# A planned attention-and-MLP kernel: engine time and result time held apart in the planner, a price for a change of matmul kind, and refitted constants

## The chip, the cores and the metric

The kernel runs on one core of one Trainium2 chip. The metric is the device time of one execution in microseconds; lower is better. An execution is one program; nothing is computed on the host but changes of layout.

## The reference

Four sequences of 448 tokens go through attention with 12 heads of 64, whose scores are mixed across heads before the softmax and again behind it, and then through two gated MLPs.

```python
scores = scale * q @ k.T                                   # (4, 12, 448, 448)
scores = einsum('bhij,hg->bgij', scores, w_pre)
attn = softmax(scores, -1)
attn = einsum('bhij,hg->bgij', attn, w_post)
x = (attn @ v), heads side by side                         # (1792, 768)
h = x @ w_in; x = (h * clip(h + 3, 0, 6) / 6) @ w_out      # d_ff 2048
x = (((x @ w1) * (x @ w2)) @ w3) @ w_out2                  # d_ff 1024
```

## The kernel before, in words

**Attention.** Query rows are cut into 16 chunks (four per sequence). For each chunk, six PE operations `scores` (two heads each) write products of q and k into PSUM; ACT or DVE copies them out into a tile `s`. For sequences 1 to 3, q and k are first split into a high and a low part by POOL (`halve`), and a scores operation is six matmuls; for sequence 0 it is two pairs. The mixes across heads work on groups of ten query rows; two groups make a slot, and there are 23 slots per sequence, 92 in all. In each slot `mix` (L460 on) does this: POOL zeroes four rows of a gather tile `g` (L472); SP issues two gathers from `s` (L481); PE multiplies by the first mixing matrix, `premix`, eight matmuls of 448 columns on 64x64 pieces of the array; DVE takes the row maximum (L495); ACT takes two exponentials with their sums (L501); POOL or DVE adds a small number to the sum, DVE takes the reciprocal and weighs the second mixing matrix with it (L517); PE does `postmix`, 64 matmuls of 60 columns; ACT and DVE copy the result into `pth` or `ptl` (L343, L345). At the end of each of eight units, `values` multiplies by v in three groups of two PE operations, 16 matmuls each. All these products take their place in four PSUM tiles (`pp`), and there are four gather tiles and four tiles `e` for the exponentials.

**The MLPs.** Here PE runs full 128x128 matmuls of 448 columns, three for each product of fp32 values split into high and low parts (`act`, `block`, `wide`, `wo`, `wb` and so on). Where two sequences are taken together, `seven` forms a 2x2 block product from seven products, with sums on DVE (`plus`, L833). The third and the fourth weight of the second MLP are multiplied with each other first (`product34`). Intermediate results go to HBM and back.

**The planner.** Nothing in this order is written out by hand. `Plan.add` collects operations with an engine (or a choice of two), a duration in ns, a priority (smaller is more urgent), what they depend on and what buffers they need. `Plan.run` then plays them through as events: whenever an engine is free, it takes the ready operation with the best priority whose buffers have room, and the kernel issues the instructions on each engine in that order. So durations, delays between engines (`HOP`, `DMA_START`, `DMA_END`, `FREED`) and the priorities' constants (`URGE`) decide the order of every queue, SP's with the DMAs among them. The chip then runs each queue in order, with its real times. The thresholds `p...` in `URGE` say how long the first engine of a choice must still be busy before the second takes the operation. `apart` keeps post-mixes from starting closer than a given time.

In the kernel before, an operation holds its engine until its result is there (`free[e] = end = now + ...`), all PE operations are alike, and PE takes the best ready one.

Of the kernel before, what the change touches and what calls it, by code (L numbers as in the profile page):

```python
# [62 lines left out]
URGE = dict(pPool=13.287, pACT=19737.186, pDVE=67509.792, pOut=3.743, pGuard=376.043, pCopy=12.835, pRest=101.643, pEvac=52.694, load0=33.466, load=-4.77, gather=-168.494, pre=-140.104, max=-8.516, exp=27.495, norm=15.87, post=2.04, evac=43.38, values=32.185, step=8.267, vload=-54.801, vload0=-30.207, lead=-15.369, begin=-9.6, consts=-75.04, moe=104.397, rows=-53.563, win=-87.391, wout=-22.784, w34=71.001, w2=99.201, unit0=3.845, unit1=6.717, down1=95.531, unit2=13.151, down2=98.964, wo=-75.16, wd=-84.964, narrow=-61.372, sums=107.353, w34us=69.981, pHalf=621.884, halve=10.141, gsum=3.533, joined=24.31, pairs=-7.78, lag=-72.907, mix=92.823, wo1=32.07)  # L63
# [26 lines left out]
class Plan:  # L90


    HOP = dict(Host=0, PE=200, ACT=150, DVE=130, Pool=130, SP=0)
    DMA_START, DMA_END, FREED = 1100, 910, 180
# [4 lines left out]
    def add(self, eng, ns, prio, emit, use=(), new=(), part=(), after=(), hold=(), read=(), chain=None, gives=None, wait=None, issue=580, port=False, apart=0):  # L99

        choice = eng if isinstance(eng, dict) else {eng: ns}
        op = dict(choice=choice, eng=None, prio=round(prio, 6), emit=emit, new=list(new), id=len(self.ops), gives=gives or {}, chain=chain, issue=issue, apart=apart, port=("Pool", "DVE") if port else ("Pool",))
# [12 lines left out]
        return op  # L118
# [12 lines left out]
    def run(self):  # L131
# [14 lines left out]
        wire = port = burst = 0.0  # L146
        freed = deque()
        events = [(0.0, -1)]
        order = []
        while events:  # L150
            now, done = heapq.heappop(events)
            if done >= 0:
                op = self.ops[done]
                for tag, n in op["gives"].items():
                    self.room[tag] += n
                for x in op["holds"]:
                    x.held -= 1
                    if not x.held:
                        freed.append((now + self.FREED, x.tag))
# [17 lines left out]
            for e, heap in waiting.items():  # L177
                if free[e] > now:
                    continue
                skipped = []  # L180
                while heap:
                    prio, i = heapq.heappop(heap)
                    op = self.ops[i]
                    if op["eng"]:
                        continue
                    first = next(iter(op["choice"]))
                    homes = None
                    if op["ready"] <= now and (e == first or free[first] > now + URGE["p" + op["wait"]]) and (port <= now or e not in op["port"]) and (not op["apart"] or burst <= now):
# [28 lines left out]
                    break  # L217
# [12 lines left out]
def attention_moe(ctx: ExitStack, tc, qd, kd, vd, consts, w_in, w_out, w1, w2, w3t, w4, out):  # L230
# [197 lines left out]
    def scores(prio, ci, hp):  # L428
# [20 lines left out]
        if b:  # L449
            op = plan.add("PE", 660, prio, emit, new=(p, *dest), hold=(st, qh, ql, kh, kl), after=(*ks[hp % 2 * 2:][:2], qs[hp * len(qs) // 6], *after))  # L450
        else:
            op = plan.add("PE", 950, prio, emit, read=(q, k), new=(p, *dest), hold=(st,), after=after)
# [9 lines left out]
    def mix(s):  # L462
# [10 lines left out]
        blanked = plan.add("Pool", 900, at + URGE["gather"] - 1, blank, new=(g,))  # L473
# [17 lines left out]
        plan.add("PE", 900, at + URGE["pre"], premix, use=(g,), new=(pre, e))  # L491
# [10 lines left out]
        for a_ in range(2):  # L502
            plan.add("ACT", 850, at + URGE["exp"], lambda a_=a_: softexp(a_), use=(pre, m, e, *((z,) if a_ else ())), new=() if a_ else (z,))
# [33 lines left out]
        op = plan.add("PE", 1020, at + URGE["post"], postmix, apart=2400, use=(e, w), new=(post, *dest), hold=(pt,), after=() if first else (pt.first,))  # L537
# [12 lines left out]
        for a_ in range(2):  # L550
            op = plan.add({"ACT": 575, "DVE": 645}, 0, at + URGE["evac"], lambda eng, a_=a_: evac(eng, a_), read=(post,), after=pt.writers[-1:] if a_ else (), hold=(pt,), wait="Evac")
            pt.writers.append(op)

    def values(prio, u, hq):
# [4 lines left out]
        for pr in range(2):  # L559
# [6 lines left out]
            plan.add("PE", 1600, prio, emit, read=(pt, v), new=() if pr else (p,), use=(p,) if pr else ())  # L566
# [116 lines left out]
    class Line:  # L683


        def weight(self, prio, src, dst=None, begun=(), raws="raw", ws="w", keep=False):
# [57 lines left out]
            plan.add({"ACT": 150 + n * 5 // 6, "DVE": 150 + n * 52 // 100}, 0, prio, high, read=(m,), new=(h, l), chain=ws if ws in ("wo", "wd") else "w", wait="Copy", port=True)  # L744
# [5 lines left out]
        def mixed(self, prio, got):  # L750
# [16 lines left out]
            for o in "cdba":  # L767
# [5 lines left out]
                a = plan.add({"ACT": 150 + n * 5 // 6, "DVE": 158 + n * 52 // 100}, 0, prio, high, after=(split[o],), new=(q,), hold=(names[o][0],), chain="w", wait="Copy", port=True)  # L773
# [96 lines left out]
    def pair_rows(prio):  # L870

        made = [(Buf("bh"), Buf("bh")) for i in range(7)]
        for c in range(KC // 2):
# [14 lines left out]
            def divide(i, n, where=where, wrote=wrote, part=part, c=c):  # L888
# [6 lines left out]
                one = plan.add({"ACT": 150 + S * 5 // 6, "DVE": 158 + S * 52 // 100}, 0, prio + c, high, after=(*wrote[n], *h.writers[:1]), new=() if c else (h, l), hold=(where[n][0], h, l), chain=None if c else "x", wait="Copy", port=True)  # L895
# [142 lines left out]
    def down(prio, dur, b, ws, graw, loaded, finish, begin, early):  # L1038
# [5 lines left out]
        for n, (k, m) in enumerate(seq):  # L1044
# [28 lines left out]
            ops.append(plan.add("PE", 607 * 4, at, emit, read=(*ws[2 * k], *ws[2 * k + 1], gh, gl), new=() if k else (p,), use=(p,) if k else (), after=() if k else (begin,)))  # L1073
# [21 lines left out]
    def combine(where, wrote, kind, n, when):  # L1095
# [7 lines left out]
        def split(o):  # L1103
# [5 lines left out]
            one = plan.add({"ACT": 150 + n * 5 // 6, "DVE": 150 + n * 52 // 100}, 0, at, high, after=wrote[o], new=(h, l), hold=(where[o][0],), chain="x", wait="Copy", port=True)  # L1109
# [92 lines left out]
    def split(prio, n, x, part, bufs, fh, fl):  # L1202
# [4 lines left out]
        one = plan.add({"ACT": 150 + n * 5 // 6, "DVE": 158 + n * 52 // 100}, 0, prio, high, after=x.writers[:1], new=bufs, hold=(x,), chain="w", wait="Copy", port=True)  # L1207
# [152 lines left out]
```

## Time and profile before

| | us |
|---|---|
| runs shown (3) | 1206.04, 1210.46, 1213.14 |
| median | 1210.46 |
| span of the profiled execution, first to last instruction | 1205.8 |
| PE busy in that span | 1175.1 (97%) |
| DVE / ACT / POOL busy | 826.0 / 625.6 / 198.0 |

The time of the profiled execution as a whole isn't given apart from its span; the span lies 0.2 us under the fastest and 4.7 us under the median run. Engines: PE is the matmul engine (TensorE), PEld its weight loads, DVE is VectorE, ACT ScalarE, POOL GpSimd, SP SyncE, which issues the DMAs. All matmuls are issued by one helper (L238), so they are told apart by the tiles they write and read: `sc` are scores, `pre` and `post` the two mixes, `val` values, `up`, `dn` and `w` the MLPs.

### The profile page before, as it was taken

The page shows a single profiled execution, that of the slowest core. Times are in us where ns is not written, and L with a number is a line of the kernel's source. Part 1 is how long each engine was busy: PE and PEld are TensorE (multiplying, and loading weights), DVE is VectorE, ACT ScalarE, POOL GpSimd, SP SyncE. Part 2 cuts the span into 40 slices and gives each one's busy share as a digit, 9 for nine tenths or more (in the row PEclk, how much of TensorE's full clock was granted, in tenths as well). Part 3 has the DMA queues.
Part 4 walks back from the last instruction along what each step waited for, and adds up shares of the span by engine and source line. Part 5 has one row for each costly group of instructions (what it writes and reads, how often), then busy time and mean ns, then how long its engine had stood idle before and what let it go on. Part 6 is the DMA issues. An engine that isn't in the chain of part 4 may idle for free.

```text
span 1205.8 us, 29514 instructions
## 1 busy us (share of the span) xinstructions
PE 1175.1 (97%) x11904; PEld 975.3 (81%) x11904; DVE 826.0 (68%) x1372; ACT 625.6 (52%) x1196; POOL 198.0 (16%) x411
## 2 busy tenths in 40 slices
PE   8999999999989999999999999999999999998998
PEld 3656665666658899999999999998899998997987
DVE  3877677776688888747855456676864578578592
ACT  7767566566666566535545443432443343334452
POOL 2575564753231000000000000000000000000000
PEclk9999999999999999999999999999999999999999
DMA  6654754745845565846989787998875438396641
GB/s 221 203 175 165 231 183 137 239 144 175 253 148 170 172 217 197 268 145 199 342 287 307 254 284 273 353 313 297 289 232 155 131 124 297 115 286 234 194 149 62
DMA packets 132945, 259.87 MB, mean 216 GB/s; under 512 B 11880, under 2 KB 75208, under 8 KB 132808
## 3 DMA queue, kind: packets, MB, share of 16 engines
q1 hardware_dynamic: 132808, 257.98, 64.7%
q8 instruction: 94, 1.54, 0.6%
q14 instruction: 43, 0.35, 0.1%
HBM read 151.97 MB, written 67.26 MB: 182 GB/s over the span
## 4 chain that ended last, share of the span: by engine, by line
PE 82%; DMA 7%; DVE 3%; ACT 3%; issue 2%; POOL 2%; SPq 2%; POOLq 0%; ACTq 0%; DVEq 0%
PE up L238 40%; PE dn L238 20%; PE w L238 6%; PE post L238 5%; PE sc L238 4%; PE val L238 4%; PE pre L238 4%; DMA g<-s 2%; DMA first<-w_in 1%; SPq L481 1%; DMA xdram<-x 1%; ACT e L501 1%; DMA qraw<-qd 1%; ACT ptl L343 1%; DMA kraw<-kd 1%
## 5 line engine op out<-in xcount | busy, mean ns | idle before, releaser
L238 PE MATMUL up<-act,block 128*128 128x448 f32 x1008 | 206.0, 366 | 5.1 <-DVE v L833 5.1
L238 PEld LDWEIGHTS up<-act,block 128*128 128x128 f32 x1008 | 190.0, 189 | 20.6 <-DVE v L833 5.8
L238 PE MATMUL dn<-gs,act 128*128 128x448 f32 x720 | 147.9, 367 | 0.0
L238 PEld LDWEIGHTS dn<-gs,act 128*128 128x128 f32 x720 | 135.2, 188 | 12.1
L238 PE MATMUL up<-act,wide 128*128 128x448 f32 x630 | 142.8, 368 | 2.0 <-POOL act L241 1.6
L238 PEld LDWEIGHTS post<-wt,e 60*64 60x64 f32 x5760 | 100.9, 135 | 50.3 <-issue 23.0
L501 ACT ACTIVATE e<-pre,m 128x448 f32<-128x448 f32 (+1 forms) x184 | 116.5, 636 | 36.5 <-DVE m L495 20.2
L495 DVE TENSOR_REDUCE m<-pre 128x2 f32<-128x896 f32 (+1 forms) x92 | 99.9, 1086 | 45.4 <-PE pre L238 45.2
L238 PEld LDWEIGHTS up<-act,wide 128*128 128x128 f32 x630 | 117.9, 188 | 13.7 <-POOL act L241 2.1
L709 ACT ACTIVATE raw<-raw 128x384 f32<-128x384 f32 (+1 forms) x140 | 72.5, 524 | 87.4 <-DMA raw<-w 37.8
L238 PE MATMUL post<-wt,e 60*64 60x60 f32 x5760 | 107.5, 220 | 6.4 <-ACT pth L343 1.6
L343 ACT CAST block<-raw 128x384 fp32r<-128x384 f32 x103 | 52.8, 514 | 110.0 <-PE up L238 72.7
L238 PE MATMUL pre<-g,wih 64*64 64x448 f32 x720 | 93.2, 562 | 4.5 <-issue 2.6
L472 POOL MEMSET g<- 4x896 f32 x92 | 76.6, 835 | 110.5 <-PE pre L238 85.4
L238 PE MATMUL up<-act,wb 128*128 128x448 f32 x432 | 89.5, 366 | 0.6 <-DVE v L833 0.5
L238 PEld LDWEIGHTS up<-act,wb 128*128 128x128 f32 x432 | 80.9, 188 | 8.4 <-DVE v L833 0.9
L241 DVE TENSOR_TENSOR block<-raw,block 128x384 fp32r<-128x384 f32 x112 | 60.5, 553 | 30.2 <-ACT block L343 30.1
L833 DVE TENSOR_TENSOR t<-up,t 128x448 f32<-128x448 f32 x60 | 37.2, 621 | 60.3 <-PE up L238 59.4
L238 PE MATMUL dn<-gs,wo 128*128 128x448 f32 x336 | 74.2, 367 | 0.0
L717 ACT ACTIVATE raw<-raw 128x768 f32<-128x768 f32 (+1 forms) x70 | 55.6, 795 | 32.0 <-DVE raw L715 31.9
L721 DVE SCALAR_TENSOR_TENSOR raw<-raw 128x384 int32<-128x384 int32 (+1 forms) x140 | 68.3, 525 | 1.2
L238 PEld LDWEIGHTS dn<-gs,wo 128*128 128x128 f32 x336 | 63.1, 188 | 5.9
(136 smaller groups left out, 1811.6 us busy)
## 6 DMA issues: line engine op xcount, KB each, us to landing
g<-s SPq DMA_DIRECT2D x180, 210.0 KB
raw<-w SPq DMA_DIRECT2D x48, 384.0 KB
graw<-g1dram SPq DMA_DIRECT2D x32, 448.0 KB
raw<-w_out SPq DMA_DIRECT2D x32, 384.0 KB
raw<-w_in SPq DMA_DIRECT2D x28, 384.0 KB
g1dram<-t SPq DMA_DIRECT2D x24, 448.0 KB
raw<-w3t SPq DMA_DIRECT2D x32, 256.0 KB
wraw<-w34dram SPq DMA_DIRECT2D x30, 256.0 KB
```

What stands on the lines that cost most here:

```text
L238: nc.tensor.matmul(o, lhsT=lt, rhs=rh, start=start, stop=stop, **kw)
L241: eng.tensor_tensor(out=o, in0=a, in1=b, op=ALU.subtract)
L343: nc.scalar.copy(o, i)
L472: nc.gpsimd.memset(g.t[:BEFORE], 0.0)
L481: nc.sync.dma_start(out=g.t[BEFORE:BEFORE + 2 * ROWS, y], in_=st.t[p0:p0 + 9 * d + 1:d])
L495: nc.vector.tensor_reduce(out=m.t[used], in_=pre.t[used, :, :S], axis=AX.X, op=ALU.max, negate=True)
L501: nc.scalar.activation(out=e.t[used, a_], in_=pre.t[used, a_, :S], func=ACTF.Exp, bias=m.t[used, a_:a_ + 1], accum_out=z.t[used, a_:a_ + 1])
L709: nc.scalar.mul(value()[:, halves[i]], f(bits(i))[:, :, 1], 2.0 ** -112)
L717: nc.scalar.activation(out=f(y), in_=f(y), func=ACTF.Prelu, alpha=-2.0 ** 32)
L721: two(out=m.t[:, halves[i]], in0=bits(i)[:, :, 0], scalar=29, in1=m.t[:, halves[i]], op0=ALU.logical_shift_right, op1=ALU.bitwise_or)
L833: return plan.add("DVE", 620, prio(at), lambda: nc.vector.tensor_tensor(out=x.t[:, k], in0=o(), in1=x.t[:, k], op=ALU.add), after=after, h ...
```

## The change

Planner: each engine has now a `LAG`, the part of a duration by which the engine is free before the result counts as there; the hops are shorter accordingly. Each PE operation has a kind (`mode`): 1 for scores, 2 for both mixes, 3 for values, 0 for the rest. An operation of another kind than the one before takes 105 ns more (`SWITCH`). When PE is free, the planner takes the best ready operation; if it is of another kind, it looks on for a ready one of the same kind with a priority at most `stay` worse, and takes that. The distance of post-mixes, 2400 ns before, is now the constant `apart`. Durations of single operations are changed, and all constants of `URGE` have new values. No operation is added or removed, and no instruction's operands are changed.

```diff
-URGE = dict(pPool=13.287, pACT=19737.186, pDVE=67509.792, pOut=3.743, pGuard=376.043, pCopy=12.835, pRest=101.643, pEvac=52.694, load0=33.466, load=-4.77, gather=-168.494, pre=-140.104, max=-8.516, exp=27.495, norm=15.87, post=2.04, evac=43.38, values=32.185, step=8.267, vload=-54.801, vload0=-30.207, lead=-15.369, begin=-9.6, consts=-75.04, moe=104.397, rows=-53.563, win=-87.391, wout=-22.784, w34=71.001, w2=99.201, unit0=3.845, unit1=6.717, down1=95.531, unit2=13.151, down2=98.964, wo=-75.16, wd=-84.964, narrow=-61.372, sums=107.353, w34us=69.981, pHalf=621.884, halve=10.141, gsum=3.533, joined=24.31, pairs=-7.78, lag=-72.907, mix=92.823, wo1=32.07)
+URGE = dict(pPool=44.724, pACT=19733.949, pDVE=67488.692, pOut=24.009, pGuard=146.25, pCopy=284.613, pRest=817.953, pEvac=117.583, load0=-688.655, load=594.158, gather=-556.042, pre=-164.891, max=45.537, exp=632.24, norm=-32.015, post=-0.851, evac=-425.937, values=110.762, step=74.946, vload=-679.584, vload0=183.522, lead=-162.891, begin=-27.935, consts=573.45, moe=335.537, rows=-292.187, win=-242.411, wout=84.104, w34=-52.685, w2=-448.231, unit0=14.449, unit1=14.524, down1=227.142, unit2=465.153, down2=496.915, wo=329.791, wd=-56.378, narrow=129.585, sums=843.42, w34us=681.355, pHalf=149.958, halve=317.445, gsum=-218.085, joined=513.339, pairs=-338.902, lag=-903.354, mix=157.29, wo1=346.91, stay=39.751, apart=2007.393)
...
-    HOP = dict(Host=0, PE=200, ACT=150, DVE=130, Pool=130, SP=0)
-    DMA_START, DMA_END, FREED = 1100, 910, 180
+    HOP = dict(Host=0, PE=230, ACT=35, DVE=35, Pool=40, SP=0)
+    LAG = dict(Host=0, PE=0, ACT=100, DVE=84, Pool=50, SP=0)
+    DMA_START, DMA_END, FREED, SWITCH = 1100, 1100, 70, 105
...
                     if "PE" in n["choice"]:
-                        hop = dict(DVE=240, PE=0).get(op["eng"], hop)
+                        hop = dict(DVE=60, ACT=55, PE=0).get(op["eng"], hop)
...
-                skipped = []
+                skipped, found = [], None
                 while heap:
                     prio, i = heapq.heappop(heap)
                     op = self.ops[i]
                     if op["eng"]:
                         continue
+                    if found and prio > found[0] + URGE["stay"]:
+                        skipped.append((prio, i))
+                        break
...
-                            homes = self.places(op["new"])
+                            if not found or op["mode"] == mode:
+                                homes = self.places(op["new"])
                     if homes is None:
                         skipped.append((prio, i))
                         continue
+                    if found:
+                        skipped.append(found[:2])
+                    found = (prio, i, homes)
+                    if e != "PE" or op["mode"] == mode:
+                        break
+                if found:
+                    _, i, homes = found
+                    op = self.ops[i]
...
-                        free[e] = end = now + op["choice"][e]
+                        end = now + op["choice"][e]
+                        if e == "PE":
+                            end += self.SWITCH if op["mode"] != mode else 0
+                            mode = op["mode"]
+                        free[e] = end - (self.LAG[e] if op["lag"] is None else op["lag"])
                         if e in op["port"]:
-                            port = end
+                            port = free[e]
...
-            op = plan.add("PE", 660, prio, emit, new=(p, *dest), hold=(st, qh, ql, kh, kl), after=(*ks[hp % 2 * 2:][:2], qs[hp * len(qs) // 6], *after))
+            op = plan.add("PE", 690, prio, emit, mode=1, new=(p, *dest), hold=(st, qh, ql, kh, kl), after=(*ks[hp % 2 * 2:][:2], qs[hp * len(qs) // 6], *after))
...
-        plan.add("PE", 900, at + URGE["pre"], premix, use=(g,), new=(pre, e))
+        plan.add("PE", 802, at + URGE["pre"], premix, mode=2, use=(g,), new=(pre, e))
...
-            plan.add("ACT", 850, at + URGE["exp"], lambda a_=a_: softexp(a_), use=(pre, m, e, *((z,) if a_ else ())), new=() if a_ else (z,))
+            plan.add("ACT", 760, at + URGE["exp"], lambda a_=a_: softexp(a_), lag=145, use=(pre, m, e, *((z,) if a_ else ())), new=() if a_ else (z,))
...
-        op = plan.add("PE", 1020, at + URGE["post"], postmix, apart=2400, use=(e, w), new=(post, *dest), hold=(pt,), after=() if first else (pt.first,))
+        op = plan.add("PE", 940, at + URGE["post"], postmix, apart=URGE["apart"], mode=2, use=(e, w), new=(post, *dest), hold=(pt,), after=() if first else (pt.first,))
...
-            plan.add("PE", 1600, prio, emit, read=(pt, v), new=() if pr else (p,), use=(p,) if pr else ())
+            plan.add("PE", 1671 if u % 2 == 0 else 1407, prio, emit, mode=3, read=(pt, v), new=() if pr else (p,), use=(p,) if pr else ())
```

Left out of the diff are like changes of other durations: the scores of sequence 0 from 950 to 752 ns, the zeroing from 900 to 840, the copies of post-mixes from 575 and 645 to 638 and 652, ACT's high parts by 45 more, and the products of the first MLP's second half from 607 to 614 ns per three matmuls.

## Rows read from the trace of the kernel before

**Rows 1.** The cores: span, mean granted clock of the matmul engine

```profile
core 0: 1205.8 us, clock 0.997
```

**Rows 2.** Four stretches: length, busy us (instructions) per engine, clock, DMA share, GB/s

```profile
0.00:360.00 360.00, 339.44 (x7713) 212.63 (x7713) 254.75 (x458) 238.24 (x547) 184.51 (x401) 1.00 0.60 190
360.00:600.00 240.00, 239.03 (x1223) 217.95 (x1224) 186.30 (x318) 138.52 (x234) 13.53 (x10) 1.00 0.63 212
600.00:1050.00 450.00, 449.05 (x2258) 410.19 (x2257) 282.27 (x468) 186.56 (x321) 0.00 (x0) 1.00 0.75 250
1050.00:1206.00 156.00, 147.56 (x713) 134.50 (x712) 102.64 (x130) 62.26 (x96) 0.00 (x0) 0.99 0.56 179
```

**Rows 3.** PE's waits: us in total, times, longest

```profile
PE up L238 <- DVE v L833: 5.5, 3, 4.1
PE sc L238 <- DMA k<-kd: 5.1, 1, 5.1
PE pre L238 <- issue: 2.6, 3, 1.8
...
PE post L238 <- ACT pth L343: 1.6, 9, 0.2
...
PE post L238 <- issue: 1.2, 2, 0.7
...
PE pre L238 <- DMA g<-s: 0.8, 1, 0.8
```

**Rows 4.** PE in order of time, attention: start, length, kind of product, idle before

```profile
5.11 12.11 PE L238 MATMUL sc<-k,u 64*120 64x448 f32 x52 [5.11 <-DMA k<-kd]
...
103.75 0.98 PE L238 MATMUL pre<-g,wih 64*64 64x448 f32 x8
104.55 1.14 PE L238 MATMUL post<-wt,e 60*64 60x60 f32 x64
105.62 0.87 PE L238 MATMUL sc<-khl,qhl 64*110 64x448 f32 x6
106.42 0.98 PE L238 MATMUL pre<-g,wih 64*64 64x448 f32 x8
...
360.13 8.66 PE L238 MATMUL val<-ptl,vv 128*64 128x208 f32 x96 [0.28 <-ACT ptl L343]
```

**Rows 5.** The same view, two scores operations side by side

```profile
228.59 1.45 PE L238 MATMUL sc<-khl,qhl 64*100 64x448 f32 x12
229.97 1.16 PE L238 MATMUL post<-wt,e 60*64 60x60 f32 x64
```

**Rows 6.** The same view, a train of mixes without scores

```profile
38.57 1.16 PE L238 MATMUL post<-wt,e 60*64 60x60 f32 x64
...
47.70 1.14 PE L238 MATMUL post<-wt,e 60*64 60x60 f32 x64
...
55.03 1.31 PE L238 MATMUL post<-wt,e 60*64 60x60 f32 x73 [0.71 <-issue]
```

**Rows 7.** ACT and DVE in order of time, attention

```profile
165.22 0.63 ACT L501 ACTIVATE e<-pre,m 128x448 f32<-128x448 f32 x1 [0.47 <-DVE m L495]
165.85 0.63 ACT L501 ACTIVATE e<-pre,m 128x448 f32<-128x448 f32 x1
...
161.40 1.09 DVE L495 TENSOR_REDUCE m<-pre 128x2 f32<-128x896 f32 x1 [0.44 <-PE pre L238]
162.40 0.65 DVE L345 COPY ptl<-post 128x480 f32<-128x480 f32 x1
```

**Rows 8.** The chain that ended last, attention: start, us, what

```profile
215.52 5.56 DMA g<-s
```

**Rows 9.** All engines in order of time, around the longest wait behind attention

```profile
1091.38 2.02 DVE L241 TENSOR_TENSOR act<-orig,act 128x1792 fp32r<-128x1792 f32 x1
...
1093.92 0.62 DVE L833 TENSOR_TENSOR v<-up,v 128x448 f32<-128x448 f32 x1
1094.59 3.59 PE L238 MATMUL up<-act,block 128*128 128x448 f32 x9 [4.12 <-DVE v L833]
```

More of the change, by code (lines that the diff above doesn't have):

```diff
@@ L449, in scores @@
         if b:
[L450 removed]
+            op = plan.add("PE", 690, prio, emit, mode=1, new=(p, *dest), hold=(st, qh, ql, kh, kl), after=(*ks[hp % 2 * 2:][:2], qs[hp * len(qs) // 6], *after))
         else:
[L452 removed]
+            op = plan.add("PE", 752, prio, emit, mode=1, read=(q, k), new=(p, *dest), hold=(st,), after=after)
         if dest:
@@ L472, in blank @@
             nc.gpsimd.memset(g.t[:BEFORE], 0.0)
-        blanked = plan.add("Pool", 900, at + URGE["gather"] - 1, blank, new=(g,))
+        blanked = plan.add("Pool", 840, at + URGE["gather"] - 1, blank, new=(g,))
         for y in both:
@@ L550, in mix @@
         for a_ in range(2):
-            op = plan.add({"ACT": 575, "DVE": 645}, 0, at + URGE["evac"], lambda eng, a_=a_: evac(eng, a_), read=(post,), after=pt.writers[-1:] if a_ else (), hold=(pt,), wait="Evac")
+            op = plan.add({"ACT": 638, "DVE": 652}, 0, at + URGE["evac"], lambda eng, a_=a_: evac(eng, a_), read=(post,), after=pt.writers[-1:] if a_ else (), hold=(pt,), wait="Evac")
             pt.writers.append(op)
@@ L743, in low @@
                 minus(e, l.t[:, :n], value(), f(h.t)[:, :n])
-            plan.add({"ACT": 150 + n * 5 // 6, "DVE": 150 + n * 52 // 100}, 0, prio, high, read=(m,), new=(h, l), chain=ws if ws in ("wo", "wd") else "w", wait="Copy", port=True)
+            plan.add({"ACT": 195 + n * 5 // 6, "DVE": 150 + n * 52 // 100}, 0, prio, high, read=(m,), new=(h, l), chain=ws if ws in ("wo", "wd") else "w", wait="Copy", port=True)
             plan.add({"DVE": 150 + n * 52 // 50, "Pool": 150 + n * 21 // 10}, 0, prio, low, read=(m, h), use=(l,), wait="Rest", port=True)
@@ L772, in high @@
                     copy(e, q.t[:, 0], part(o))
-                a = plan.add({"ACT": 150 + n * 5 // 6, "DVE": 158 + n * 52 // 100}, 0, prio, high, after=(split[o],), new=(q,), hold=(names[o][0],), chain="w", wait="Copy", port=True)
+                a = plan.add({"ACT": 195 + n * 5 // 6, "DVE": 158 + n * 52 // 100}, 0, prio, high, after=(split[o],), new=(q,), hold=(names[o][0],), chain="w", wait="Copy", port=True)
                 b = plan.add("DVE", 150 + n * 52 // 50, prio, lambda q=q, o=o: minus("DVE", q.t[:, 1], part(o), f(q.t)[:, 0]), after=(a,), hold=(names[o][0], q), port=True)
@@ L894, in high @@
                     copy(e, h.t[:, c], part(n))
-                one = plan.add({"ACT": 150 + S * 5 // 6, "DVE": 158 + S * 52 // 100}, 0, prio + c, high, after=(*wrote[n], *h.writers[:1]), new=() if c else (h, l), hold=(where[n][0], h, l), chain=None if c else "x", wait="Copy", port=True)
+                one = plan.add({"ACT": 195 + S * 5 // 6, "DVE": 158 + S * 52 // 100}, 0, prio + c, high, after=(*wrote[n], *h.writers[:1]), new=() if c else (h, l), hold=(where[n][0], h, l), chain=None if c else "x", wait="Copy", port=True)
                 two = plan.add("DVE", 150 + S * 52 // 50, prio + c, lambda: minus("DVE", l.t[:, c], part(n), f(h.t)[:, c]), after=(one,), hold=(where[n][0], h, l), port=True)
@@ L1072, in emit @@
                         mm(p.t[:, q, :S], w[1].t[:, c], gh.t[:, i], False, k == K - 1 and i == 1)
-            ops.append(plan.add("PE", 607 * 4, at, emit, read=(*ws[2 * k], *ws[2 * k + 1], gh, gl), new=() if k else (p,), use=(p,) if k else (), after=() if k else (begin,)))
+            ops.append(plan.add("PE", 614 * 4, at, emit, read=(*ws[2 * k], *ws[2 * k + 1], gh, gl), new=() if k else (p,), use=(p,) if k else (), after=() if k else (begin,)))
             if k == K - 1:
@@ L1108, in high @@
                 copy(e, h.t, part(o))
-            one = plan.add({"ACT": 150 + n * 5 // 6, "DVE": 150 + n * 52 // 100}, 0, at, high, after=wrote[o], new=(h, l), hold=(where[o][0],), chain="x", wait="Copy", port=True)
+            one = plan.add({"ACT": 195 + n * 5 // 6, "DVE": 150 + n * 52 // 100}, 0, at, high, after=wrote[o], new=(h, l), hold=(where[o][0],), chain="x", wait="Copy", port=True)
             two = plan.add("DVE", 150 + n * 52 // 50, at, lambda: minus("DVE", l.t, part(o), f(h.t)), after=(one,), hold=(where[o][0], h, l), port=True)
@@ L1206, in high @@
             copy(e, fh(), part())
-        one = plan.add({"ACT": 150 + n * 5 // 6, "DVE": 158 + n * 52 // 100}, 0, prio, high, after=x.writers[:1], new=bufs, hold=(x,), chain="w", wait="Copy", port=True)
+        one = plan.add({"ACT": 195 + n * 5 // 6, "DVE": 158 + n * 52 // 100}, 0, prio, high, after=x.writers[:1], new=bufs, hold=(x,), chain="w", wait="Copy", port=True)
         two = plan.add("DVE", 150 + n * 52 // 50, prio, lambda: minus("DVE", fl(), part(), f(fh())), after=(one,), hold=(x, *bufs), port=True)
```

6 lines of the change are left out of this document (3 added, 3 removed).

## The prediction

> **What bounds the kernel now.** Read the cores first: one core, a span of 1205.8 us at a granted clock of 0.997 of full speed [rows 1]. The three runs shown have a median of 1210.46 (1206.04 to 1213.14); the profiled execution is at their lower end. My sum is made against its span, and its difference is carried to the median.
>
> The busy time by stretches comes next [rows 2]. The matmul engine PE is busy 339.4 of the first 360 us (attention), 239.0 of the next 240, 449.1 of 450, and 147.6 of the last 156. So PE bounds everything, and the 690 us in the middle have 1.9 us of idle. No operand or matmul count changes in the diff, so only two things can give time: idle PE, and PE time that is busy without working. Idle PE is 20.6 us in attention and 8.4 in the last stretch. No other engine is near its limit in attention: DVE 255 of 360, ACT 238, POOL 185, DMA 0.60.
>
> The list of PE's waits [rows 3] says what the idle is: 5.1 for the first load of k, 5.5 for a DVE addition at L833 (4.1 of it in one piece), many small waits behind copies out of PSUM (one row has nine, of 1.6 us together), and 3.8 us of "issue", for which the profile shows no releaser.
>
> The busy part that does no work shows in PE's timeline. In the steady state each slot goes scores, pre-mix, post-mix [rows 4]: a post-mix starts 0.80 us after its pre-mix (same kind), the scores 1.07 after that, the next pre-mix 0.80 later. Where two scores operations stand together they take 1.38 us, 0.69 each [rows 5]. A single one occupies 0.80, so a change of kind costs about 0.11 us. From the first to the last row of PE's timeline in rows 4 there are 309 groups and, by the four kinds of the diff, 225 changes of kind: 225 x 0.11 = 25 us.
>
> **The change, part by part.**
>
> *Prefer the kind that just ran.* The planner looks past the best ready PE operation for one of the same kind whose priority is at most 39.751 worse. A slot is 14.449 of the new units, so that is 2.75 slots. How many changes go? The pattern has two per slot; a pair of scores followed by two pre- and post-mixes would halve it, and the two halves of a values operation, mostly apart now, would join. I take 100 fewer. Bounds: none (nothing of the same kind is ready), and 145 fewer (24 values groups and 16 scores chunks, each one run with a change before and behind it, leave 80). What is one worth? The 0.11 of the scores is the upper end. The lower end is the early train without scores [rows 6]: five post-and-pre cycles take 47.70 - 38.57 = 9.13 us, 1.826 each, against 0.80 + 1.07 = 1.87 in the steady state, so the switch left out brought only 0.04. I take 0.08, between the two because scores and values join as well as mixes: 100 x 0.08 = **-8 us**; bounds 0 and 145 x 0.11 = -16.
>
> *Post-mixes at least 2.007 us apart instead of 2.4.* Just behind that train PE stands 0.71 us with no releaser [rows 6]; each post-mix is 64 small matmuls. In the steady state a cycle of 0.80 + 1.07 + 0.80 = 2.67 us lies between two [rows 4], so the bound seldom binds. The train's 1.826 against a planned 802 + 940 = 1.742 is 0.084 per pair. If all 92 slots ran so, 92 x 0.084 = 7.7 us would be lost against plan; the price of a switch above already has it, so I add 0 and keep +4 (half the slots) as a bound. The Trainium skill, "Runtime: NRT & Kernel Launch", section "Instruction fetch mechanics", says that instruction fetch is hidden because dispatch is slower than the refill; by that rule the denser spacing would cost nothing and the sum would be 100 x 0.03 = 3 us lower, as every switch would bring the full 0.11. The train and the issue waits speak against it, if fetch is what they are; the profile doesn't say.
>
> *Engine time and result time apart.* Before, an exponential held ACT for 850 ns in the plan. In the trace the next starts 0.63 us after it; the new plan holds ACT for 760 - 145 = 615. A row maximum holds DVE for 1.00 us from start to start though its row says 1.09 [rows 7]; the new plan has 1080 - 84 = 996, the old 1080. So the new figures match the chip, and the old plan believed ACT much fuller than it is. A plan on true figures should lose some of the idle that stands in attention beside the first load: 20.6 - 5.1 = 15.5 us, of which 3.8 is issue and not in the model. I take **-3 us**. Bounds: -9 (most of the rest), and +6, as the old overstatement was also slack against late transfers, and less slack turns lateness into waits.
>
> *Refitted priorities.* They reorder every queue, SP's and POOL's among them. In the middle 690 us PE has no idle to win; cover there is deep, and I count 0. At the end, one wait of 4.12 us stands [rows 9]: a split of 2.02 us on DVE was ordered ahead of the addition that the last product of a step waits for. With unit2 at 465 and gsum at -218, that split outranks the step's last sums by number too, so I don't count on its going: 0, with -4.6 and +8 (two more such stalls) as ends. The constants now rank behind five input loads. The first scores run until 17.2 us [rows 4] and the first load is in at 5.1; four more loads are 1.6 MB, at the 190 GB/s of rows 2 8.5 us, so the constants are there by about 14: 0, and a few us if that cover goes. Costs of the planner itself (hops, durations) emit no instruction: 0.
>
> Sum: -8 - 3 = **-11 us**, a span of 1195 and 1210.5 - 11 = **1199.5 us** for the median.
>
> **The rivals.** A difference of 0.5%, 6 us, is what a measurement here can tell from no change.
>
> *PSUM paces the runs (about the same).* All attention products share four PSUM tiles. A run of pre-mixes, 0.80 us each on PE, needs a row maximum each, 1.00 on DVE [rows 7]; longer runs than the buffers cover are then paced at 1.00, a loss of 0.2 per further pre-mix, twice the switch saved. Then only the -3 remains: 1207.5. For it: the small waits of PE behind PSUM copies [rows 3] show that buffers already run out at moments. Against: DVE and ACT are 66 to 71% busy in attention [rows 2], and the plan models the four tiles. The Trainium skill, "TensorEngine Tiling (Array Packing)", section "PSUM Bottleneck", warns of just this, that a faster TensorE leaves the PSUM copy as the bound. No row here shows it for whole stretches.
>
> *The preference finds nothing.* If two of one kind are seldom ready together, changes of kind stay near 225, and 1207.5 results as well. The pairs that already occur by chance [rows 5] speak against it.
>
> *Slower: gathers late at the change of a query chunk.* A pre-mix needs its gather from the scores tile, and its first gather of a chunk needs all six scores operations copied out. The plan gives a gather 1.25 + 1.10 + 1.10 = 3.45 us; on the chain of waits it stood 5.56 [rows 8]. Four gather tiles at 360/92 = 3.9 us per slot cover 15.6 us. A turn takes a pre-mix 0.8, a zeroing and two issues of about 0.8 each, and 5.5 of landing, 8.7 in all, which leaves 7 us. Behind a late gather stand, on SP, the next loads and the stores of x, and on POOL, whose zeroing waits for a gather tile, the halving of the next q and k. Scores held back by the full 2.75 slots, 10.8 us, would overrun that by 3.8. On half of the 14 chunks after the first two, that is 27 us: 1199.5 + 27 = 1226. It decides from 11/14 = 0.8 us of wait per chunk (no gain left), and is a loss over 0.5% from 1.2. Against: now only 0.8 us of PE's idle is put to a gather, and the planner knows the dependence, if not its full length.
>
> **How the numbers follow.** Forecast 0.72, of which 0.04 ends within 0.5%; PSUM pacing 0.10; nothing found 0.06; late gathers 0.12. So faster 0.68, same 0.20, slower 0.12. The forecast's own bounds go from -16 - 9 in attention and -4.6 behind it to about +5; both ends at once are unlikely, and I cut the lower end at 1187, -23. Upward the range takes in the two neutral cases and a mild form of the late gathers, to 1215. Some 0.1 is left out above and 0.07 below.
>
> **What would show it.** Right: the four kinds change clearly less often in attention (about 125 times), the values halves stand as groups of 32, attention ends 8 to 14 us earlier, and the stretches from there to 1050 keep their lengths. PE's matmul count and busy time after attention stay. Wrong: waits of PE on DVE's row maximum or on PSUM copies that grow by what the switches saved (pacing); waits of the pre-mix on g of over 10 us in sum (late gathers); issue over 8 us (spacing); or new idle between 600 and 1206, where I assume none.

## The result and the profile after

The kernel after takes 1221.65 us (median of 9 runs, 1215.61 to 1224.19), the kernel before 1211.63 beside it (9 runs, 1206.04 to 1217.95). The ratio is 1.0066, interval 1.0041 to 1.0091: slower, by about 8 us (the medians lie 10.0 apart), where 1199.5 was forecast. The 1221.65 lies above the upper end of the range, 1215.

The cores of the profiled execution, against [rows 1]:

```profile
core 0: 1222.4 us, clock 0.990
```

The four stretches, against [rows 2]:

```profile
0.00:360.00 360.00, 333.78 (x7601) 210.06 (x7602) 230.74 (x420) 251.02 (x571) 177.62 (x392) 0.97 0.60 188
360.00:600.00 240.00, 236.61 (x1285) 212.79 (x1284) 192.36 (x328) 144.21 (x247) 16.62 (x13) 1.00 0.63 208
600.00:1050.00 450.00, 445.69 (x2216) 403.33 (x2215) 272.33 (x438) 188.14 (x317) 0.00 (x0) 1.00 0.73 248
1050.00:1222.00 172.00, 164.76 (x808) 150.82 (x806) 110.68 (x145) 70.28 (x112) 0.00 (x0) 1.00 0.55 180
```

PE's idle is the length less the busy time. It was 20.6, 1.0, 0.9 and 8.4; it is 26.2, 3.4, 4.3 and 7.2: in all 30.92 before and 41.16 after, **10.2 us more**, of which 5.8 lie in the 690 us in the middle. The granted clock of the first stretch fell from 1.00 to 0.97. Over the span, the clock lost is 1205.8 x 0.003 = 3.6 us before and 1222.4 x 0.010 = 12.2 after, **8.6 us more**. PE's timeline has 226 changes of kind before and 205 after; 21 x 0.11 = **2.3 us less**. The sum, 10.2 + 8.6 - 2.3 = 16.5, is the difference of the two spans, 16.6; as the clocks are given to a thousandth, 1.2 us of a span, agreement to 0.1 us is in part luck.

This pair of executions overstates the clock's part. Span x (1 - granted clock), worked out for every run, is 9.8 us in the median run of after and 5.4 to 7.3 in those of before; the time without it is 1211.9 after and 1205.1 to 1207.1 before. So the clock makes some 3 us of the difference of the medians. That waits make the rest is read from the profiled pair alone.

PE's waits, against [rows 3]:

```profile
PE up L255 <- DVE v L850: 5.7, 2, 2.9
PE sc L255 <- DMA k<-kd: 5.1, 1, 5.1
PE post L255 <- issue: 4.0, 4, 2.3
PE pre L255 <- issue: 3.9, 4, 1.8
PE post L255 <- DVE wt L534: 3.3, 5, 2.1
PE val L255 <- DVE s L362: 3.0, 1, 3.0
PE post L255 <- DVE pth L362: 2.4, 1, 2.4
PE up L255 <- ACT t L847: 2.2, 3, 1.1
```

The old long waits stand (first load, addition for v), and new ones of about 2 us came into attention: "issue" went from 3.8 to 7.9, and post-mixes and a values product wait for DVE. PE in order of time shows five of these waits, the same values product once more at full speed, and attention's last values:

```profile
35.01 0.90 PE L255 MATMUL post<-wt,e 60*64 60x60 f32 x42 [2.29 <-issue]
...
48.04 1.16 PE L255 MATMUL post<-wt,e 60*64 60x60 f32 x64 [2.12 <-DVE wt L534]
...
61.86 0.60 PE L255 MATMUL pre<-g,wih 64*64 64x448 f32 x4 [1.83 <-issue]
...
87.95 3.47 PE L255 MATMUL val<-pth,vv 128*64 128x240 f32 x16 [2.96 <-DVE s L362]
...
94.75 1.84 PE L255 MATMUL val<-pth,vv 128*64 128x240 f32 x16
...
230.18 1.98 PE L255 MATMUL post<-wt,e 60*64 60x60 f32 x64 [2.39 <-DVE pth L362]
...
365.29 8.66 PE L255 MATMUL val<-ptl,vv 128*64 128x208 f32 x96
```

The values product at 87.95 takes 3.47 us, the same at 94.75 takes 1.84: behind the wait PE works for a while at the lower level, 1.2 GHz. Attention ends at 373.95, 5.2 us later than before [rows 4].

### The profile page after: what moved, and what is told of

Its sections match the earlier page's. It is cut to its first block, busy times and chain, and to the rows that moved or that the text cites. A ratio compares the mean times of both kernels' runs of the same rounds, so it can differ in the third digit from the quotient of the medians.

```text
span 1222.4 us, 29442 instructions
## 1 busy us (share of the span) xinstructions
PE 1180.8 (97%) x11904; PEld 977.0 (80%) x11904; DVE 806.1 (66%) x1330; ACT 653.6 (53%) x1245; POOL 194.2 (16%) x404
## 4 chain that ended last, share of the span: by engine, by line
PE 80%; DVE 7%; DMA 6%; issue 3%; ACT 3%; POOL 1%; SPq 0%; DVEq 0%; POOLq 0%; ACTq 0%
PE up L255 34%; PE dn L255 17%; PE post L255 6%; PE val L255 6%; PE pre L255 5%; PE sc L255 5%; PE w L255 5%; DMA raw<-w_out 1%; DMA raw<-w 1%; DMA g<-s 1%; DMA raw<-jadram 1%; DVE raw L738 1%; DMA raw<-w_in 1%; ACT raw L734 1%; DVE act L258 1%
## 5 line engine op out<-in xcount | busy, mean ns | idle before, releaser
L255 PE MATMUL up<-act,block 128*128 128x448 f32 x1008 | 208.7, 369 | 5.7 <-DVE v L850 5.7
L255 PE MATMUL dn<-gs,act 128*128 128x448 f32 x696 | 150.5, 367 | 0.6 <-DVE gs L258 0.6
L255 PEld LDWEIGHTS dn<-gs,act 128*128 128x128 f32 x696 | 130.6, 188 | 12.7 <-DVE gs L258 0.9
L255 PEld LDWEIGHTS up<-act,wide 128*128 128x128 f32 x645 | 120.4, 188 | 13.9 <-ACT v L847 1.5
L360 ACT COPY s<-sc 120x896 f32<-120x896 f32 (+2 forms) x75 | 67.8, 905 | 23.2 <-PE sc L255 23.0
```

The costliest lines, as they stand in the source:

```text
L255: nc.tensor.matmul(o, lhsT=lt, rhs=rh, start=start, stop=stop, **kw)
L360: nc.scalar.copy(o, i)
```

## The experiments

p9 to p13 keep an order and add work to it; the others have an order of their own, and the table gives three figures for each. *Plan* is the end that the kernel's own planner expects when it has ordered everything. *Chip* is the median over the runs of the time less the lost clock as above. *Gap* is chip minus plan. The chip figure of before is taken over the 73 runs beside p1 to p14; with the 19 beside p15 to p17 it would be 1206.2.

| kernel | edit | plan | ratio to before | chip | gap |
|---|---|---|---|---|---|
| before | | 1197.7 | 1 | 1205.6 | 7.9 |
| after | | 1177.1 | 1.0066 [1.0041, 1.0091] | 1211.9 | 34.8 |
| p1 | after, spacing 2.3 us | 1179.7 | 1.0053 [1.0033, 1.0073] | 1208.7 | 29.0 |
| p2 | before, preference alone | 1209.7 | 1.0127 [1.0098, 1.0157] | 1217.0 | 7.3 |
| p3 | after, constants of before | 1188.1 | 1.0033 [1.0003, 1.0062] | 1208.8 | 20.7 |
| p4 | after, costs of before | 1215.2 | 1.0197 [1.0160, 1.0235] | 1223.4 | 8.2 |
| p5 | before, spacing 2.007 us | 1200.1 | 0.9998 [0.9975, 1.0022] | 1206.5 | 6.4 |
| p6 | before, constants off by up to 0.2% | 1199.2 | 1.0027 [1.0007, 1.0047] | 1207.7 | 8.5 |
| p7 | after, exponential planned at 840 ns | 1188.4 | 1.0209 [1.0138, 1.0279] | 1219.8 | 31.4 |
| p8 | after, lags a tenth smaller | 1187.5 | 1.0129 [1.0097, 1.0162] | 1217.2 | 29.7 |
| p14 | after, spacing 2.5 us | 1186.2 | 1.0163 [1.0120, 1.0207] | 1215.2 | 29.0 |
| p15 | p2 with PE's new costs | 1208.7 | 1.0089 [1.0061, 1.0117] | 1212.7 | 4.0 |
| p16 | p2 with all the other new costs | 1189.6 | 1.0064 [1.0036, 1.0092] | 1214.2 | 24.6 |
| p17 | p2 with all new costs | 1204.9 | 1.0213 [1.0156, 1.0271] | 1219.6 | 14.7 |

**One part at a time (p1 to p4).**

```diff
# p1, from after
-apart=2007.393
+apart=2300
# p2, from after: old URGE, old durations, HOP, FREED, DMA_END; LAG and SWITCH 0
+stay=6, apart=2400
# p3, from after: old URGE
+stay=10.577, apart=2400
# p4, from after: old durations, HOP, FREED, DMA_END; LAG and SWITCH 0
```

> The changed kernel with one constant changed: post-mixes at least 2.3 us apart in the plan instead of 2.007; the plan's own end stays within 3 us (1177.1 to 1179.7 us). Theory A (the refitted plan has no slack: every disturbance becomes a wait of PE, and PE waits of about 2 us are followed by a stretch at the lower clock level): still slower than the kernel before, ratio 1.003 to 1.011. Rival C (dense post-mixes starve PE of instructions): issue before PE falls from 7.9 us to under 4, fewer lower-clock stretches in the first 100 us, ratio 0.997 to 1.003. Rival B (preferring the kind that just ran makes PE wait): no change against the changed kernel, 1.005 to 1.009.

> The kernel before plus the preference alone (stay 6 in the old units, that is 1.6 slots): old costs, old constants, 2.4 us spacing. 198 changes of kind planned instead of 226; the plan's own end is 1209.7 against 1197.7 us for the kernel before. Rival B: slower than before, ratio 1.005 or more, with PE waits on DVE's row maximum or on copies out of PSUM. Theory A: the preference itself is harmless and saves 28 x 0.1 = 3 us, but this plan has 12 us more of planned time, part of it slack that the chip doesn't use: 0.995 to 1.006.

> The changed planner (new costs, price of a change of kind, preference over 2.75 slots) with the old constants and 2.4 us spacing. 191 changes of kind planned; the plan's own end is 1188.1 us, 9.6 under the plan of the kernel before. Theory A (the new constants, fitted to the plan's own clock, are what makes it slower): ratio 0.994 to 1.003, early PE waits of 2 us or more gone. Rival B or D (the new costs or the preference are to blame): 1.004 or more, with lower-clock stretches in the first 100 us.

> The new constants and the preference, but the old costs: hops, durations, an engine held until its result is there, no price of a change of kind. The plan's own end by those costs is 1215.2 us, 17.5 over the kernel before. Theory A with the blame on the new costs (they take the slack out of the plan): 0.997 to 1.004, and few lower-clock stretches. If the constants are to blame whatever the costs: 1.005 to 1.015.

Each part moved the whole order, so none is a clean subtraction. The wider spacing of p1 left 7.0 us of issue waits (7.9 in after), so rival C's "under 4" fell. The preference alone made the kernel 1.27% slower, with 198 changes of kind in place of 226: the chip gave its plan's loss (12.0 us) back as 11.4. Its issue waits rose from 3.8 to 9.9 us. The new costs on the old constants end 3.2 us over before (chip) where their plan promised 9.6 less. New constants under the old costs are worst, as their plan says.

**Spacing and chance (p5, p6).**

```diff
# p5, from before
-apart=2400
+apart=2007
# p6, from before: every number of URGE times a factor drawn from 0.998 to 1.002
```

> The kernel before with post-mixes allowed 2.007 us apart instead of 2.4, nothing else; the plan's own end is 1200.1 against 1197.7 us. Rival C (dense post-mixes starve PE): issue before PE above 6 us (3.8 before) and ratio 1.004 or more. Theory A (it is the lost slack of the whole plan, not the spacing): issue about as before, ratio 0.998 to 1.005.

> A control: the kernel before with every constant moved by at most 0.2%, which means nothing; the plan's own end is 1199.2 against 1197.7 us. If orders that the plan rates alike take alike on the chip: 0.998 to 1.004. If the chip scatters by itself among like plans: anything from 0.995 to 1.012, and then a difference of 0.7% between two refits needs no deeper cause than which order was drawn.

Closer post-mixes alone cost nothing, though the issue waits of the profiled execution rose to 6.5 us. A meaningless change of the constants cost 0.27% in the one draw that was run: an order as such can be worth that much.

**Is the new order brittle on ACT (p7 to p10)?** Theory A said that the new plan leaves ACT no slack.

```diff
# p7, from after
-            plan.add("ACT", 760, at + URGE["exp"], ...
+            plan.add("ACT", 840, at + URGE["exp"], ...
# p8, from after (and lag=145 to lag=130)
-    LAG = dict(Host=0, PE=0, ACT=100, DVE=84, Pool=50, SP=0)
+    LAG = dict(Host=0, PE=0, ACT=90, DVE=76, Pool=45, SP=0)
# p9, from before, and p10, from after: the order unchanged, in softexp
+            if a_:
+                nc.scalar.copy(spare[:, :64], wih[:, :64])
```

> The changed kernel with the exponential planned at 840 instead of 760 ns, so that ACT has some slack; the plan's own end is 11.3 us worse (1188.4 against 1177.1). Theory A (the 1177 of the plan is a sharp optimum that the chip can't follow): on the chip not slower than the changed kernel, ratio to before 1.000 to 1.007, fewer waits of PE of 2 us or more. If the plan ranks orders rightly: 1.012 or more.

> The changed kernel with nine tenths of each lag (engine free 10% later relative to the result: 90, 76, 45 and 130 ns), a change of at most 15 ns per operation; the plan's own end is 10.4 us worse (1187.5). Theory A: 0.999 to 1.008. If the plan ranks rightly: 1.012 or more.

> The kernel before, in its own order, with one small copy more on ACT behind the second exponential of each slot (128x64 to an unused tile, 92 in all, about 0.2 us each, 18 us of ACT in all, which the plan doesn't know). Theory A (the order before has slack that takes up such disturbances): at most 4 us slower, ratio 0.999 to 1.004. Rival (both orders are equally tight): as much slower as the changed kernel is with the same copy.

> The changed kernel in its own order with the same small copy on ACT. Theory A (the refitted order uses ACT without slack): 6 to 14 us slower than the changed kernel without it, so ratio to before 1.012 to 1.020. Rival (both equally tight, or both loose): the same difference as in the kernel before.

Theory A fell twice. The two plans that cost ACT or the results later are later by 11.3 and 10.4 us, and their kernels are slower by 17.4 and 5.4 (medians; 7.9 and 5.3 by the chip figure). And 92 more copies on ACT cost neither order anything: p9 0.999 [0.9957, 1.0024], p10 1.0039 [1.0002, 1.0076] against before, no more than after itself.

**What a wait of 2 us costs (p12), and filling such waits (p11).**

```diff
# p12, from before, at the first step of each down product; copies = 0, 2, 4 in turn
+                    if copies:
+                        mm(p.t[:, 0, :S], ws[0][0].t[:, col(2 * m)], gh.t[:, 0], True, True)
+                    for _ in range(copies):
+                        nc.vector.tensor_copy(p.t[:, 0, :S], p.t[:, 0, :S])
# p11, from after
+            if s in (7, 57):
+                fill(post)
...
+                    if (u, hq) == (0, 2):
+                        fill(p)
```

> The kernel before with 16 waits of PE made on purpose in its densest part (first step of 16 down products): a matmul into the product's tile, two or four copies of 448 columns of that tile onto itself on DVE (0.6 us each), then the product as before. Eight waits of about 1.4 us and eight of about 2.6 us, 32 us of waiting, and 16 extra matmuls of 0.2, 3 us. Theory B: behind each long one stands a stretch at half the granted clock, 1.7 us lost in each, behind the short ones none: 32 + 3 + 14 = 49 us, ratio 1.040. Rival 1 (the clock has no part): 35 us, 1.029. Rival 2 (PE's lead over the loads and copies is won back in such a wait, as the planned idle in before's order was): less than 25 us, below 1.020.

> The kernel after, its order unchanged, with eight matmuls whose result is overwritten (64 rows, 448 columns, 1.6 us in all) put ahead of three operations that stood 2.12, 2.96 and 2.39 us in the trace of after (the post-mixes of slots 7 and 57 and the third values product of unit 0), each followed by 3.4 or 6.8 us in which the granted clock was half. Theory B (a wait of 2 us costs its own length and as much again of lost clock): the fillers run inside the waits, the half-clock stretches behind them go, 1.7 + 3.4 + 1.7 = 6.8 us less, about 1215, ratio to before 1.001 and below 1.004. Rival 1 (the clock falls whatever PE does there, or the waits stand elsewhere in other runs): the fillers are added work, 3 x 1.6 = 4.8 us more, 1.010. Rival 2 (what is saved is lost at the next wait): 1.006 as before the edit.

There are 12 such places, so four waits of each length came, not eight. PE in order of time around the first two, and two windows behind (length, busy of the five engines, clock, DMA share, GB/s):

```profile
585.79 1.50 PE L238 MATMUL dn<-gs,early 128*128 128x448 f32 x6 [1.39 <-DVE dn L1071]
587.13 1.40 PE L238 MATMUL dn<-gs,wo 128*128 128x448 f32 x6
...
591.45 1.49 PE L238 MATMUL dn<-gs,early 128*128 128x448 f32 x6 [2.73 <-DVE dn L1071]
592.78 2.33 PE L238 MATMUL dn<-gs,wo 128*128 128x448 f32 x6
```

```profile
593.00:596.00 3.00, 3.00 (x9) 2.65 (x8) 3.00 (x6) 1.96 (x4) 0.00 (x0) 0.50 0.77 184
596.00:600.00 4.00, 4.00 (x20) 3.66 (x19) 2.48 (x5) 0.84 (x1) 0.00 (x0) 0.96 0.60 231
```

Behind the wait of 1.39 us six matmuls take 1.40, behind the one of 2.73 the same six take 2.33, with the clock at 0.50. All four long waits were followed so, none of the four short ones. The lost clock of its four runs is 13.0 us on average against 6.3 in before's: 6.7 / 4 = **1.7 us per long wait, on top of its length**. It isn't the price of every such wait: behind after's wait of 2.92 us at 1112.45 the clock stayed at 1.00 (1112.5 to 1120). The rest fits too: 4 x 1.39 + 4 x 2.73 = 16.5 and 8 matmuls of 0.2 make 18.1, and the chip figure rose from 1206.3 to 1225.3, by 19.0. The ratio, 1.0199 [1.0156, 1.0243], speaks for theory B against rival 1 when both are halved to 12 places: 24.5 us (1.020) against 17.5 (1.014). Rival 2, below 12.5 us when halved, fell.

The fillers of p11 brought the clock back where they stand. First a window of after around the values product at 87.95; then the filler, the same product, which stands earlier in p11, and a window around them:

```profile
86.00:97.00 11.00, 9.05 (x60) 4.60 (x64) 5.52 (x10) 2.80 (x7) 5.45 (x14) 0.69 0.01 2
```

```profile
80.47 1.74 PE L255 MATMUL val<-wih 64*64 64x448 f32 x16
82.13 1.84 PE L255 MATMUL val<-pth,vv 128*64 128x240 f32 x16
```

```profile
80.00:84.00 4.00, 4.00 (x42) 1.82 (x42) 3.51 (x5) 1.84 (x4) 3.44 (x8) 1.00 0.58 201
```

But the whole stayed at 1221.4, 1.0078 [1.0047, 1.0110]: theory B's 1.001 fell. The lost clock shrank by 1.3 us on average and the time without it rose by 4.0, about the fillers' own 3 x 1.7. The waits had moved:

```profile
PE post L255 <- issue: 9.9, 9, 2.7
```

**What an issue wait is (p13), and a wider spacing (p14).**

```diff
# p13, from before, ahead of the 12 down products
+                    for _ in range((1, 2, 4, 8)[len(trains) % 4]):
+                        for a_ in range(2):
+                            for n in range(8):
+                                for y in range(2):
...
+                                    mm(p.t[o, y, c0:c0 + ROWS], f(gh.t)[i, 0, 48 * n:48 * n + 64], f(gh.t)[i, 1, :ROWS], True, True)
# p14, from after
-apart=2007.393
+apart=2500
```

> The kernel before with trains of 1, 2, 4 or 8 post-mixes' worth of matmuls back to back (64 small ones each, 64 rows by 60 columns), three of each length, put ahead of 12 down products; their result is overwritten. One post-mix alone occupies 0.96 us where the next operation is of its kind. Theory C (the waits without a releaser come from a supply of instructions that dense trains of small matmuls outrun): a train of 1 or 2 takes 0.96 us each, those of 4 and 8 take clearly more than 3.9 and 7.7 us, with waits marked issue of some tenths to two us inside. Rival (the supply keeps up, and the issue waits have another cause, such as a wait that the profile can't place): 0.96 us each at every length, 7.7 for eight, and no issue wait in these trains. The whole gets longer by 45 x 0.96 = 43 us by the rival, by more under C.

> The kernel after with its post-mixes at least 2.5 us apart in the plan in place of 2.007. The plan's own end is 9.1 us later than that of after (1186.2 for 1177.1). Theory C (dense post-mixes outrun the supply of instructions, and each such wait brings half-clock stretches): issue waits fall from 7.9 to about 4, stretches at half clock from 7 to 3 or 4, and the time to 1213 to 1217, ratio to before 1.001 to 1.005, although the plan is later. Rival (the plan's end decides, as it ranked the others within one cost model): 9 us more than after, 1231, ratio 1.014.

PE in order of time in p13, a train of two post-mixes and one of eight:

```profile
590.89 2.09 PE L238 MATMUL dn<-gs 60*64 60x60 f32 x128
...
609.41 3.02 PE L238 MATMUL dn<-gs 60*64 60x60 f32 x190
613.58 2.09 PE L238 MATMUL dn<-gs 60*64 60x60 f32 x128 [1.15 <-issue]
617.05 2.09 PE L238 MATMUL dn<-gs 60*64 60x60 f32 x128 [1.38 <-issue]
620.52 1.25 PE L238 MATMUL dn<-gs 60*64 60x60 f32 x66 [1.38 <-issue]
```

The first 190 run at 16 ns each, then PE stands, and from there on every 128 take 617.05 - 613.58 = 3.47 us, 37 per us, whatever PE could do. Trains of four took 8.1 to 9.6 us in place of 3.9, those of eight 12.3 to 16.6 in place of 7.7 (the longest in part at the lower clock), those of one 1.09, and one of the three of two was late (2.90):

```profile
PE dn L238 <- issue: 28.2, 14, 4.5
```

The trace's DMA packets show what PE waits for here. The page of p13 has this line (packets, MB, share):

```profile
q8 instruction: 116, 1.90, 0.6%
```

Each of these packets is 16,384 bytes. The 14,784 matmuls of p13 and as many weight loads make 255 of PE's instructions per packet, so 128 small matmuls with their weight loads are one packet's worth. All 14 waits above end a whole number of 256 PE instructions apart from each other (to within one), 1.2 to 1.6 us behind the end of such a packet (packets from 614.69 to 615.81 and from 618.17 to 619.10; PE goes on at 617.05 and 620.52). So PE waits there for its own instructions. Of the seven issue waits over 0.3 us in after, six end in the same way, 6.7 of 7.7 us, that at 35.01 among them (packet from 32.21 to 33.52); so does the wait of 0.71 us in [rows 6].

The whole took 1301.29 us in its one run, 90 more than before's, for 43 us of added work: theory C holds for trains. A post- and a pre-mix are 72 matmuls; at the train of [rows 6], 1.826 us, that is 39 per us, just over those 37; with a scores operation between, 78 in 2.67 us, 29 [rows 4]. So a train of mixes without scores should just outrun the supply, and a mixed order not. As a cure by spacing the theory fell: p14 has the same 7.9 us of issue, and its time went with its plan, 9.1 us later there and 7.7 in the median on the chip (3.3 without the lost clock).

**Which of the new costs (p15 to p17).** The table's last column had shown the pattern: every kernel planned with the old costs ended 6.4 to 8.5 us behind its plan, every one with the new costs 20.7 to 34.8.

```diff
# p15, from p2: PE's durations and SWITCH of after
# p16, from p2: HOP, LAG, FREED, DMA_END and all durations but PE's of after
# p17, from p2: both
```

> The kernel before's constants with the preference (6 of its units, as in p2) and the new durations of PE and price of a change of kind; hops, lags and the durations of the other engines as before. The plan's end is 1208.7. Taken off each run's time: the clock it lost (span x (1 - granted clock)). What is left stood 6 to 9 us over the plan's end in every kernel planned with the old costs, 21 to 35 over it with the new ones. Theory D (the new hops, lags and durations off PE make the plan too rosy): 6 to 9 over the plan here, so 1215 to 1218 without the lost clock, about 1223 with it, ratio 1.009 to 1.013. Rival (PE's new durations do): 18 to 25 over it, 1227 to 1234 without, ratio 1.018 or more.

> As p15 the other way round: PE's durations as before and no price for a change of kind, but the new hops, lags and durations of ACT, DVE, POOL and the DMAs. The plan's end is 1189.6. Theory D: 18 to 25 us over it, 1208 to 1215 without the lost clock, ratio 1.003 to 1.009. Rival: 6 to 9 over it, 1196 to 1199, ratio 0.992 to 0.995, which would beat the kernel before.

> The same constants and preference with all the new costs. The plan's end is 1204.9. If the gap belongs to the costs and not to the order that a search found, it is 18 to 25 us here too: 1223 to 1230 without the lost clock, ratio 1.015 to 1.021. If it belongs to orders that were searched for with those costs, 6 to 12 us, 1211 to 1217, ratio 1.005 to 1.010.

p16 has the gap, 24.6; p15 has none, 4.0 (less than either theory gave). From p2 to p16 the plan gets 20.1 us shorter and the chip 2.8: theory D holds. What these costs make worse here is the plan and not the kernel. p17, at 14.7, lies between what was expected of the costs and of the search, so the gap grows with orders that were searched for under these costs (34.8 for after, 20.7 for p3), but this one run doesn't fix by how much.

Rows of after show the kind of thing that the new figures leave out. DVE and ACT in order of time:

```profile
154.16 0.27 DVE L534 TENSOR_TENSOR wt<-wip,r 128x120 f32<-128x120 f32 x1
...
163.04 1.08 DVE L512 TENSOR_REDUCE m<-pre 128x2 f32<-128x896 f32 x1
...
172.19 0.73 DVE L534 TENSOR_TENSOR wt<-wip,r 128x120 f32<-128x120 f32 x1
```

```profile
164.23 0.64 ACT L518 ACTIVATE e<-pre,m 128x448 f32<-128x448 f32 x1 [1.55 <-DVE m L512]
```

From a row maximum's start to its exponential's, 164.23 - 163.04 = 1.19 us pass; the new plan has 1080 + 35 = 1115 ns, the old one had 1080 + 130 = 1210. A weighing planned at 250 ns in both takes 0.27 in one row and 0.73 in the other; the mean of all is 317 ns, in before as in after. Whether such terms make the whole gap was not tried one by one. By the planner's own times the last values product ends at 347.0 us in after and at 364.6 in before; on the chip it ended at 373.95 and 368.79. So 26.9 us of the gap stand at the end of attention in after, 10.2 of them lost clock, and 4.2 in before, 1.7 of them lost clock.

## Why the prediction was wrong, point by point

- **"Prefer the kind that just ran": -8.** The size failed first. "I take 100 fewer" was 21 fewer, 2.3 us at my price, close to the rival that finds nothing. And the preference isn't free: alone it costs 11.4 us (p2, with a setting of 6 that was not searched for), and in its profiled execution the issue waits are 6.1 us longer. Part of that may be the price of any order that was not searched for: lags smaller by at most 15 ns cost the plan 10.4 us too (p8). My lower price of a change, 0.04, came from a train that the supply of instructions held back, and so says little of a change of kind.
- **"Engine time and result time apart": -3.** Here the sign failed. "A plan on true figures should lose some of the idle": idle rose by 10.2 us. I compared single figures (0.63 for an exponential, 1.00 for a row maximum) and they do match. But those matches leave the sum of a plan 25 us too early (p16), where the old overstatement left it a steady 6 to 9 behind. So the search under them found a plan 20.6 us shorter and a kernel that is 6.3 longer (chip). That the new costs by themselves make a kernel slower is not shown: no run has them without the preference, and beside it p16 ended before p2. My upper bound named this ("the old overstatement was also slack") and gave it +6; p7 to p10 show that it isn't slack on ACT.
- **"Post-mixes at least 2.007 us apart": 0, bound +4.** Right for the part by itself (p5). The mechanism that I left open is real: trains outrun a supply of 37 small matmuls per us (p13). The Trainium skill, "Runtime: NRT & Kernel Launch", section "Instruction fetch mechanics", has fetch hidden behind dispatch; the packets show that these waits are for fetch, so the trains, 12.3 to 16.6 us in place of 7.7, disagree, and the measurement decides.
- **"Refitted priorities": 0.** In the middle I had no idle to win and gave nothing to lose: it lost 5.8 us, its own new waits of up to 2.8 us among them. The long wait for v behind attention went from 4.12 to 2.92, and the same row's sum stayed (5.5 and 5.7).
- **A term that the sum hadn't:** lost clock. Idle was priced at its length; a wait of 2.73 us cost 4.4 in p12. In the profiled pair that is 8.6 us, in the medians some 3.
- **The rivals.** No wait of PE on a gather is among the long ones: late gathers fell. Waits behind copies out of PSUM (s, pth, ptl: 3.0, 2.4 and 2.0 us) did grow, but as single events, not as the pacing of whole runs. That it could end slower was right, by another mechanism, which no rival of mine held. Both terms of the sum failed: the -8 gave 2.3 us and brought waits of its own, and the -3 had the wrong sign. The experiments don't divide the loss between the two.

## What to carry to other kernels

Judge a planner's cost model by how steadily the chip ends behind the plan over several orders, not by how well each figure matches a row: the model with cruder figures kept the same distance from the chip, and a search under the sharper one bought 20.6 us that only the plan saw. Price a wait of PE with the clock that it can lose, and count trains of small matmuls against the rate at which they can be supplied.

## What the runs showed of the hardware

Small matmuls (64 rows by 60 columns) ran at 16 ns each for the first 190 of the train shown, then at 128 in 3.47 us, one instruction packet of 16,384 bytes for each 128. In that stretch a packet started 1.1 us after PE had gone on, took 0.9 to 1.1, and PE went on 1.2 to 1.4 behind its end. Four waits of PE of 2.73 us were each followed by a stretch at half the granted clock that cost 1.7 us more; four of 1.39 us by none, and one of 2.92 us in after by none either. The spread between runs is in part the same thing: of after's nine runs, three at a clock of 0.996 average 1216.9 us and five at 0.990 to 0.992 average 1223.0, 6.0 more, while the clock lost differs by some 6.6.

Why the packet that the refitted order waits for at 35 us started only at 32.21, and which single cost makes its plan too early, stays open. No version tried beats the kernel before.
